# A Winograd convolution whose first unit begins with points 0 and infinity, with the third weight loaded behind the rows

## The chip, the cores and the metric

The kernel runs on one core of a Trainium2 chip. The metric is the device time in microseconds of one launch. The kernel before takes 189.95 us (median of three runs, 189.86 to 190.31).

## The reference

A convolution of width 3 over the sequence, with 1024 channels in and out, for two sequences of 2048 positions, then batch normalization and SiLU. Everything is bf16 in memory.

```python
B, S, C, K = 2, 2048, 1024, 3
xp = jnp.pad(x, ((0, 0), (1, 1), (0, 0)))
y = sum(jnp.einsum('bsc,cd->bsd', xp[:, k:k + S, :], w[k]) for k in range(K))
inv_std = 1.0 / jnp.sqrt(var + 1e-5)
y = (y - mean) * (g * inv_std) + b
return jax.nn.silu(y)
```

## The kernel before

The kernel computes the convolution by a Winograd scheme: six outputs (R) at a time from eight transformed inputs (NJ), one for each of the points 0, 1, -1, 2, -2, 1/2, -1/2 and infinity. A sequence has 342 blocks of six positions (NB). Channels stand in 8 tiles of 128 on either side (CT in, DC out).

**Loading.** SP loads the rows of x in 17 windows of up to 128 rows for each sequence (L486 to L489 and L505), 256 KB each but for the short one that comes first, into 12 buffers. The three weights of output tile 0 (256 KB each: the tap planes 0, 2 and 1 in this order) stand in SP's queue behind windows number 5, 8 and 11 (W0_AT). Eight semaphores serve all loads in turn, and a load waits for the one eight places before it.

**Transform of x.** `t_jobs` makes 25 jobs for a sequence. A job (`t_job`, L270) is a group of matmuls of the rows with the matrix `rm` (L278), which put the eight transformed inputs of some blocks into PSUM, and one cast into `T_sb` in SBUF by ScalarE (L289) or VectorE (L291). Which of the two does it is planned at build time: `clock` and `cost` keep an estimate of when each engine is free, and the job goes to the one that would end first. `ahead` (L491) does all jobs of sequence 0 before the first product; those of sequence 1 are strewn among the products of unit 0 by `Between` (L510), 23 of them after so many products as match their share of columns, and the last two by `rest`.

**Transform of the weights.** For an output tile GpSimd makes three pairs `u`: u0 = e0 ± w1, with e0 = w0 + w2, for the points ±1; u1 = e1 ± 2 w1, with e1 = w0 + 4 w2, for ±2; and u2 = e2 ± 2 w1, with e2 = 4 w0 + w2, for ±1/2. Points 0 and infinity take the raw planes w0 and w2. In tile 0 (`prepare_first`, L208) GpSimd does all sums, and ScalarE scales by 4 and 2; it is called behind job 16 of sequence 0. For the other tiles (`prepare_w`, L192) GpSimd makes e0 and the pairs (L169, L190), ScalarE doubles w1 (L157), and VectorE makes e1 and e2 (L171), handed out by `idle` at set places of a unit.

**Units.** A unit (L300) is one output tile and one sequence; there are 16, in the order (tile 0, sequence 0), (tile 0, sequence 1), (tile 1, sequence 0) and so on, and they use PSUM banks 0 to 3 and 4 to 7 by turns. A unit makes eight products, each of 8 matmuls of 128x342 (`product`, L316, its matmuls at L324). `run` (L380) has the order of the first six: points 1, 2, -1, -2, then 1/2 and -1/2. Behind them ScalarE copies some banks to SBUF (L335, L337), and VectorE combines them (L342): `sd`, then a combine into bank 1, then t0, t1 and t2, and, after the last two products, the combines that leave the six outputs in PSUM and in t1. The products of infinity (`last`) and of point 0 (`first`) are added into banks 3 and 0 at the very end of a unit, in the course of the next unit (`rest`), in which ScalarE also does the SiLU of the unit before. The first unit gets `between.rest` instead. `prepare_w` for the next tile is called within `run`, behind the t combines; the first unit prepares tile 1, which unit 2 is the first to use.

The order on each engine is the order in which the program issues the instructions: each engine works through its own queue, with semaphores between them. Ahead of everything six matmuls on zeros (L74) keep TensorE busy until x arrives.

Of the kernel before, what the change touches and what calls it, by code (L numbers as in the profile page):

```python
# [9 lines left out]
ALU = mybir.AluOpType  # L10
FP32 = mybir.dt.float32
BF16 = mybir.dt.bfloat16
# [3 lines left out]
P = 128  # L16
R = 6
NJ = 8
W0_AT = (5, 8, 11)
W0_USE = 16  # L20
EARLY = 23
XBUFS = 12
WARM = 6
WT = 21

@with_exitstack
def kernel(
# [10 lines left out]
    nc = tc.nc  # L38
    B, S, C = x.shape
    D = w.shape[2]  # L40
    CT, DC = C // P, D // P
    NB = -(-S // R)
# [4 lines left out]
    consts = ctx.enter_context(tc.tile_pool(name="consts", bufs=1))  # L47
# [17 lines left out]
    ps = pspool.tile([P, 8, 512], FP32, name="ps")  # L65
# [2 lines left out]
    rows = consts.tile([4 * DC, P], BF16, name="rows")  # L68
    for q, ap in enumerate((var, g, mean, b)):
        nc.scalar.dma_start(out=rows[q * DC:(q + 1) * DC, :], in_=ap.rearrange("(dc p) -> dc p", p=P))  # L70
    zeros = consts.tile([P, 512], BF16, name="zeros")
    nc.vector.memset(zeros, 0.0)
    for _ in range(WARM):
        nc.tensor.matmul(ps[:, 7], lhsT=zeros[:, 0:P], rhs=zeros, start=True, stop=True)  # L74
# [30 lines left out]

    rm = transform_matrix()

    clock = {"pe": 3500.0, "act": 0.0, "dve": 0.0, "dma": 2600.0}
    cost = {"act": (0.833, 250.0), "dve": (1.042, 215.0)}
    bank_free = {}  # L110

# [3 lines left out]
    def busy(e, size):  # L115
        clock[e] = ends(e, size)
# [4 lines left out]
    def load_x(bi, wi):  # L121
        xw = xpool.tile([P, C], BF16, name="xw")
        lo = max(R * WT * wi - 1, 0)
        hi = min(lo + P, S)
        nc.sync.dma_start(out=xw[0:hi - lo, :], in_=x[bi, lo:hi, :])  # L125
        clock["dma"] += 5.7 * (hi - lo)
        xwin[bi, wi] = xw, clock["dma"]

    w_all = w.rearrange("k (ct p) d -> p k ct d", p=P)
    raw, wts = {}, {}  # L130
# [3 lines left out]
    def load_w(pair, k, half=None):  # L134

        if (pair, "tile") not in raw:
            raw[pair, "tile"] = wpools[pair % 2].tile([P, 3, CT, 2, P], BF16, name=f"wch{pair % 2}")
        wch = raw[pair, "tile"]
        h0, h1 = (0, 2) if half is None else (half, half + 1)
        cols = slice((2 * pair + h0) * P, (2 * pair + h1) * P)  # L140
        nc.sync.dma_start(  # L141
            out=wch[:, k, :, h0:h1].rearrange("p c h d -> p c (h d)"), in_=w_all[:, k, :, cols]
        )
        clock["dma"] += 1200.0 * (h1 - h0)
        for h in range(2):
            raw[2 * pair + h] = wch[:, :, :, h]

    double, sums, act_work, dve_work = {}, {}, [], []

    def idle(work):  # L150
        if work:
            work.pop(0)()

    def double_w(dc, eng):
        t = spool.tile([P, CT, P], BF16, name="w1x2")
        if eng is nc.scalar:
            nc.scalar.mul(t, raw[dc][:, 1], 2.0)  # L157
            busy("act", CT * P)
        else:
            eng.tensor_scalar(t, raw[dc][:, 1], 2.0, 0.0, op0=ALU.mult, op1=ALU.add)  # L160
        double[dc] = t

    def even_part(dc, q, eng, by=None):

        w0, w2 = raw[dc][:, 0], raw[dc][:, 2]
        e = epool.tile([P, CT, P], FP32, name=f"e{q}")
        f, h = (w2, w0) if q == 1 else (w0, w2)
        if q == 0:
            eng.tensor_tensor(e, w0, w2, op=ALU.add)  # L169
        elif eng is nc.vector:  # L170
            eng.scalar_tensor_tensor(out=e, in0=f, scalar=4.0, in1=h, op0=ALU.mult, op1=ALU.add)  # L171
        else:
            t = spool.tile([P, CT, P], BF16, name="w1x2")
            if by is nc.scalar:
                by.mul(t, f, 4.0)
                busy("act", CT * P)
            else:
                by.tensor_scalar(t, f, 4.0, 0.0, op0=ALU.mult, op1=ALU.add)
            eng.tensor_tensor(e, t, h, op=ALU.add)
        if eng is nc.vector:  # L180
            busy("dve", CT * P)
        sums[dc, q] = e

    def transform_w(dc, q, signs=(0, 1)):

        o = double[dc] if q else raw[dc][:, 1]
        if (dc, q) not in wts:
            wts[dc, q] = upool.tile([P, 2, CT, P], BF16, name=f"u{q}")
        for i in signs:
            nc.gpsimd.tensor_tensor(wts[dc, q][:, i], sums[dc, q], o, op=(ALU.add, ALU.subtract)[i])  # L190

    def prepare_w(dc):  # L192

        even_part(dc, 0, nc.gpsimd)
        transform_w(dc, 0)

        def second():
            even_part(dc, 1, nc.vector)
            transform_w(dc, 1)

        def third():
            even_part(dc, 2, nc.vector)
            transform_w(dc, 2)

        act_work.append(lambda: double_w(dc, nc.scalar))
        dve_work.extend((second, third))

    def prepare_first(dc):  # L208

        even_part(dc, 0, nc.gpsimd)  # L210
        transform_w(dc, 0, (0,))
        even_part(dc, 1, nc.gpsimd, nc.scalar)
        double_w(dc, nc.scalar)
        transform_w(dc, 1, (0,))
        transform_w(dc, 0, (1,))
        transform_w(dc, 1, (1,))
        even_part(dc, 2, nc.gpsimd, nc.gpsimd)
        transform_w(dc, 2)

    prm = consts.tile([P, 4, DC], BF16, name="prm")  # L220
    scale = consts.tile([P, DC], FP32, name="scale")
# [78 lines left out]
    class Unit:  # L300
# [64 lines left out]
        def both(self, between, then):  # L365
# [3 lines left out]
            self.product(3, NJ - 1, True, between)  # L369
            self.silu(slice(0, R, R - 1), ps[:, self.b0:self.b0 + 4:3, self.lo:self.hi])  # L370

        def rest(self, between, last=5, first=6):
# [113 lines left out]
    for i, wi in enumerate(order):  # L486
        load_x(0, wi)
        if i in W0_AT:
            load_w(0, (0, 2, 1)[W0_AT.index(i)], 0)  # L489

    def ahead(jobs, job_n):  # L491
        for job in jobs:
            t_job(job, job_n % 4 * 2)
            if job_n == 0:
                first_matrix()
            if job_n == 2:
                params()
            if job_n == 5:
                scales()
            if job_n == W0_USE:  # L500
                prepare_first(0)
            job_n += 1

    ahead(t_jobs(0), 0)
    for wi in order:  # L505
        load_x(1, wi)
    for k in (0, 2, 1):
        load_w(0, k, 1)

    class Between:  # L510


        n = done = cols = 0
        jobs = list(t_jobs(1))
        size = [len(wins) * nct * n for wins, _, n, _, nct in jobs]

        def do(self):
            t_job(self.jobs[self.done], (4, 6, 1)[self.done % 3] if self.done < EARLY else (6, 4)[(self.done - EARLY) % 2])
            self.cols += self.size[self.done]
            self.done += 1  # L520

        def __call__(self):
            self.n += 1
            while self.done < EARLY and self.cols * 4 * CT < min(self.n, 4 * CT) * sum(self.size[:EARLY]):
                self.do()

        def rest(self):
# [3 lines left out]
    between = Between()  # L531
    seq = [(dc, bi) for dc in range(DC) for bi in range(B)]
    late = [nc.sync] * (S // R // P + 1) + [nc.gpsimd]
    before = prev = None
    for i, (dc, bi) in enumerate(seq[:-1]):
        unit = Unit(dc, bi, i % 2 * 4)
        unit.run(
            between, prev.rest(between, *((4, 5) if i >= len(seq) - 3 else (5, 6))) if prev else [(5, between.rest)],
            1 if i == 0 else 2 if i == 2 else dc + 2 if bi == 1 and 0 < dc < DC - 2 else None,
        )  # L540
        if i == 0:
            xwin_scope.close()
# [12 lines left out]
    before.store(late)  # L555
    dc, bi = seq[-1]
# [45 lines left out]
```

## Time and profile before

| | |
|---|---|
| median of 3 runs | 189.95 us |
| the profiled execution | 190.66 us, its span 188.9 us |
| TensorE busy (matmuls) | 177.3 us, 94% of the span |
| VectorE | 155.4 us, 82% |
| GpSimd | 139.7 us, 74% |
| ScalarE | 111.1 us, 59% |
| DMA | 31.72 MB, 168 GB/s on average |
| matmuls of the products, L324 | 816 with u and 272 with the raw planes, 120.9 and 42.5 us busy |

The page gives busy time by engine and by group of instructions (engine, line, operation, tiles), the median time of one, and what ended the idle time before it. PE is TensorE, PEld its weight loads, DVE is VectorE, ACT is ScalarE, POOL is GpSimd, and SPq is the queue of SP. A line of a timeline has the start in us, the length in us, the engine, the line of the code, the operation, its tiles as out<-in with sizes, the count of like instructions that it merges, and, in brackets, how long the engine was idle before it and for whom. A line of the chain of waits has the start, the length and the work or wait. A matmul's row is longer than the spacing of matmuls, since they overlap.

### The profile page before, as it was taken

The page shows a single profiled execution, that of the slowest core. Times are in us where ns is not written, and L with a number is a line of the kernel's source. Part 1 is how long each engine was busy: PE and PEld are TensorE (multiplying, and loading weights), DVE is VectorE, ACT ScalarE, POOL GpSimd, SP SyncE. Part 2 cuts the span into 40 slices and gives each one's busy share as a digit, 9 for nine tenths or more (in the row PEclk, how much of TensorE's full clock was granted, in tenths as well). Part 3 has the DMA queues.
Part 4 walks back from the last instruction along what each step waited for, and adds up shares of the span by engine and source line. Part 5 has one row for each costly group of instructions (what it writes and reads, how often), then busy time and mean ns, then how long its engine had stood idle before and what let it go on. Part 6 is the DMA issues. An engine that isn't in the chain of part 4 may idle for free.

```text
span 188.9 us, 3725 instructions
## 1 busy us (share of the span) xinstructions
PE 177.3 (94%) x1404; PEld 125.2 (66%) x1404; DVE 155.4 (82%) x214; ACT 111.1 (59%) x180; POOL 139.7 (74%) x83
## 2 busy tenths in 40 slices
PE   7767799999999999999999999999999999999981
PEld 3646588776666666666666666666666666669880
DVE  5545978789988899998799989888979997669781
ACT  3777887974547474546545654656455546363790
POOL 3536999984798879999999999889999773020122
PEclk9999999999999999999999999999999999999998
DMA  5999999247053939399669584996595768876935
GB/s 164 295 327 353 371 348 243 45 141 199 17 108 29 182 66 201 111 253 205 114 131 185 113 173 139 225 209 127 116 208 110 155 56 183 154 142 131 202 73 111
DMA packets 86958, 31.72 MB, mean 168 GB/s; under 512 B 73542, under 2 KB 82778, under 8 KB 86940
## 3 DMA queue, kind: packets, MB, share of 16 engines
q1 hardware_dynamic: 85820, 31.24, 74.0%
q10 hardware_dynamic: 864, 0.21, 0.5%
q8 instruction: 11, 0.18, 0.4%
q0 software_dynamic: 256, 0.03, 0.2%
q14 instruction: 7, 0.06, 0.1%
HBM read 14.82 MB, written 8.39 MB: 123 GB/s over the span
## 4 chain that ended last, share of the span: by engine, by line
PE 84%; DMA 9%; DVE 1%; SPq 1%; ACT 1%; issue 1%; ACTq 0%; DVEq 0%
PE ps L324 78%; DMA xw<-in_x_dram 7%; PE ps L278 5%; DMA rows<-in_g_dram 1%; DVE T_sb L291 1%; PE ps L436 1%; SPq L125 1%; ACT T_sb L289 1%; SPq L141 0%; ACTq L70 0%; ACT yT L347 0%; DVEq L597 0%; DVE o L437 0%; DVEq L291 0%
## 5 line engine op out<-in xcount | busy, mean ns | idle before, releaser
L324 PE MATMUL ps<-T_sb,u 128*128 128x342 bf16 (+2 forms) x816 | 120.9, 299 | 0.4 <-ACT T_sb L289 0.4
L324 PEld LDWEIGHTS <-u 128*128 128x128 bf16 x816 | 76.7, 97 | 33.5 <-issue 0.2
L190 POOL TENSOR_TENSOR u<-e,w1x 128x1024 bf16<-128x1024 f32 x32 | 70.3, 2220 | 9.5 <-DVE e L171 9.3
L324 PE MATMUL ps<-T_sb,wch 128*128 128x342 bf16 (+2 forms) x272 | 42.5, 300 | 0.0
L347 ACT ACTIVATE yT<-ps,beta,scale 128x342 bf16<-128x342 f32 (+4 forms) x50 | 33.9, 710 | 11.9 <-PE ps L324 11.8
L342 DVE SCALAR_TENSOR_TENSOR t<-ps,sd 128x684 f32<-128x684 f32 (+2 forms) x51 | 39.1, 821 | 0.6
L190 POOL TENSOR_TENSOR u<-e,wch 128x1024 bf16<-128x1024 f32 x16 | 36.7, 2312 | 1.7 <-DMA wch<-in_w_dram 1.1
L324 PEld LDWEIGHTS <-wch 128*128 128x128 bf16 x272 | 25.7, 97 | 11.5
L335 ACT COPY pc<-ps 128x342 f32<-128x342 f32 (+2 forms) x34 | 14.5, 425 | 31.7 <-PE ps L324 30.9
L291 DVE CAST T_sb<-ps 128x1008 bf16<-128x1008 f32 (+2 forms) x20 | 21.7, 1103 | 11.6 <-PE ps L278 11.2
L278 PE MATMUL ps<-rm,xw 128*128 128x168 bf16 (+2 forms) x272 | 25.9, 239 | 5.3 <-DMA xw<-in_x_dram 4.7
L289 ACT CAST T_sb<-ps 128x1008 bf16<-128x1008 f32 (+2 forms) x30 | 25.2, 873 | 7.3 <-PE ps L278 6.6
L342 DVE SCALAR_TENSOR_TENSOR ps<-ps,t 128x684 f32<-128x684 f32 (+2 forms) x34 | 28.3, 831 | 0.6
L171 DVE SCALAR_TENSOR_TENSOR e<-wch 128x1024 f32<-128x1024 bf16 x14 | 28.7, 2048 | 0.0
L278 PEld LDWEIGHTS <-xw 128*128 128x128 bf16 (+2 forms) x272 | 21.0, 100 | 11.1 <-DMA xw<-in_x_dram 6.5
L342 DVE SCALAR_TENSOR_TENSOR ps<-ps,pc 128x342 f32<-128x342 f32 (+2 forms) x34 | 16.9, 497 | 8.7 <-PE ps L324 5.7
L169 POOL TENSOR_TENSOR e<-wch 128x1024 f32<-128x1024 bf16 x8 | 19.0, 2371 | 4.6 <-DMA wch<-in_w_dram 3.1
L347 ACT ACTIVATE yT<-t,beta,scale 128x684 bf16<-128x684 f32 (+2 forms) x17 | 15.7, 925 | 0.0
L342 DVE SCALAR_TENSOR_TENSOR t<-ps,t 128x684 f32<-128x684 f32 (+2 forms) x17 | 13.9, 818 | 0.0
L335 ACT COPY sd<-ps 128x342 f32<-128x342 f32 (+2 forms) x17 | 7.3, 428 | 10.1 <-PE ps L324 9.7
L337 ACT ACTIVATE pc<-ps 128x342 f32<-128x342 f32 (+2 forms) x17 | 7.5, 440 | 9.8 <-PE ps L324 6.0
L478 POOL DMA_DIRECT2D out_dram<-o x2 | 1.4, 710 | 15.4 <-DMA o<-yT 15.4
(46 smaller groups left out, 49.1 us busy)
## 6 DMA issues: line engine op xcount, KB each, us to landing
xw<-in_x_dram SPq DMA_DIRECT2D x32, 256.0 KB
out_dram<-o SPq DMA_DIRECT2D x28, 192.0 KB
wch<-in_w_dram SPq DMA_DIRECT2D x9, 512.0 KB
out_dram<-o SPq DMA_DIRECT2D x14, 120.0 KB
wch<-in_w_dram SPq DMA_DIRECT2D x6, 256.0 KB
out_dram<-o SPq DMA_DIRECT2D x3, 128.0 KB
o<-yT SPq DMA_TRANSPOSE x15
out_dram<-o SPq DMA_DIRECT2D x12, 7.5 KB
```

The costliest lines, as they stand in the source:

```text
L125: nc.sync.dma_start(out=xw[0:hi - lo, :], in_=x[bi, lo:hi, :])
L169: eng.tensor_tensor(e, w0, w2, op=ALU.add)
L171: eng.scalar_tensor_tensor(out=e, in0=f, scalar=4.0, in1=h, op0=ALU.mult, op1=ALU.add)
L190: nc.gpsimd.tensor_tensor(wts[dc, q][:, i], sums[dc, q], o, op=(ALU.add, ALU.subtract)[i])
L278: nc.tensor.matmul(v[:, q, c], lhsT=xw[0:rows, (c0 + c) * P:(c0 + c + 1) * P], rhs=mat[0:rows, :, 0:n], start=True, stop=True,)
L289: nc.scalar.copy(dst, src)
L291: nc.vector.tensor_copy(dst, src)
L324: nc.tensor.matmul(self.bank[q], lhsT=lhsT, rhs=T_sb[self.bi][:, ct, j, nsl], start=not add and ct == 0, stop=ct == CT - 1, skip_group_che ...
L335: nc.scalar.copy(dst, self.bank[q])
L337: nc.scalar.mul(dst, self.bank[q], by)
L342: nc.vector.scalar_tensor_tensor(out=out, in0=in0, scalar=scalar, in1=in1, op0=ALU.mult, op1=op1)
L347: nc.scalar.activation(self.yT[:, rows, self.lo:self.hi], src, ACT.Silu, bias=beta[:, dc:dc + 1], scale=scale[:, dc:dc + 1])
```

## The change

The third weight plane (w1) of output tile 0 stands in SP's queue behind all rows of sequence 0 instead of behind window 11. `prepare_first` is split. Its first half is called behind job 5: GpSimd makes 4 w0, e0, 4 w2 and e1, which need planes 0 and 2 alone. The rest (`left`: the pairs, the doubling of w1 on ScalarE, and e2) is issued at the start of unit 0.

Unit 0 has an order of its own, `run_first`: its first two products are points 0 and infinity, with raw planes, each copied by ScalarE to an SBUF tile `ends`; then the six others as in `run`. GpSimd adds the two copies onto one half of t0 and of t2, behind VectorE's combines that make these and ahead of `prepare_w` for tile 1. VectorE makes t2 ahead of t1. In unit 1 nothing of unit 0 is left but SiLU work (`rest_first`).

The jobs of sequence 1 follow a table (`at`): the first behind 8 matmuls, then at 12, 14, 16, 18, 20, 22, and the others evenly up to 48. Some figures of the planner differ (3600, 5.4, 1400, T_FIRST). The zeros are fp32, and two matmuls on them take the place of six in bf16.

```diff
-W0_AT = (5, 8, 11)
-W0_USE = 16
+W0_AT = (5, 8, 16)
-WARM = 6
+T_FIRST = 21500.0
+WARM = 2
-    zeros = consts.tile([P, 512], BF16, name="zeros")
+    zeros = consts.tile([P, 512], FP32, name="zeros")
-    clock = {"pe": 3500.0, "act": 0.0, "dve": 0.0, "dma": 2600.0}
+    clock = {"pe": 3500.0, "act": 0.0, "dve": 0.0, "dma": 3600.0}
-        clock["dma"] += 5.7 * (hi - lo)
+        clock["dma"] += 5.4 * (hi - lo)
-        clock["dma"] += 1200.0 * (h1 - h0)
+        clock["dma"] += 1400.0 * (h1 - h0)
     def prepare_first(dc):
-        even_part(dc, 0, nc.gpsimd)
-        transform_w(dc, 0, (0,))
-        even_part(dc, 1, nc.gpsimd, nc.scalar)
-        double_w(dc, nc.scalar)
-        transform_w(dc, 1, (0,))
-        transform_w(dc, 0, (1,))
-        transform_w(dc, 1, (1,))
-        even_part(dc, 2, nc.gpsimd, nc.gpsimd)
-        transform_w(dc, 2)
+        w0, w2 = raw[dc][:, 0], raw[dc][:, 2]
+        g, f = (spool.tile([P, CT, P], BF16, name="w1x2") for _ in range(2))
+        nc.gpsimd.tensor_scalar(f, w0, 4.0, 0.0, op0=ALU.mult, op1=ALU.add)
+        for q, t, h in ((0, w0, w2), (1, g, w0)):
+            if q:
+                nc.gpsimd.tensor_scalar(g, w2, 4.0, 0.0, op0=ALU.mult, op1=ALU.add)
+            sums[dc, q] = epool.tile([P, CT, P], FP32, name=f"e{q}")
+            nc.gpsimd.tensor_tensor(sums[dc, q], t, h, op=ALU.add)
+        def left():
+            transform_w(dc, 0, (0,))
+            double_w(dc, nc.scalar)
+            transform_w(dc, 1, (0,))
+            transform_w(dc, 0, (1,))
+            transform_w(dc, 1, (1,))
+            sums[dc, 2] = epool.tile([P, CT, P], FP32, name="e2")
+            nc.gpsimd.tensor_tensor(sums[dc, 2], f, w2, op=ALU.add)
+            transform_w(dc, 2)
+        return left
+        def run_first(self, between, left, prepare):
...
+            left()
+            self.product(3, 0, False, between)
+            self.copy(3, dst=ends[:, 0])
+            self.product(0, NJ - 1, False, between)
+            self.copy(0, dst=ends[:, 1])
+            clock["pe"] = max(clock["pe"], T_FIRST)
+            self.product(3, 1, False, between)
+            pa = self.copy(3)
+            self.product(0, 3, False, between)
+            pb = self.copy(0, by=4.0)
+            self.product(3, 2, True, between)
+            self.copy(3, dst=sd[:, 0])
+            self.combine(sd[:, 1], pa, 2.0, b3, ALU.subtract)
+            self.product(0, 4, True, between)
+            self.combine(b1, b0, -2.0, pb)
+            for t, a in ((t0, -0.0125), (t2, -0.2), (t1, -0.05)):
+                self.combine(t, self.low, a, sd)
+            nc.gpsimd.tensor_tensor(t0[:, 0], t0[:, 0], ends[:, 0], op=ALU.add)
+            nc.gpsimd.tensor_tensor(t2[:, 1], t2[:, 1], ends[:, 1], op=ALU.add)
+            prepare_w(prepare)
+            self.product(2, 5, False, between)
+            pc = self.copy(2)
+            between.rest()
+            self.product(2, 6, True, between)
+            self.combine(b3, b2, -0.5, pc)
...
+        def rest_first(self):
+            return [
+                (4, self.silu_inner),
+                (5, lambda: self.silu(slice(0, R, R - 1), ps[:, self.b0:self.b0 + 4:3, self.lo:self.hi])),
+            ]
     def ahead(jobs, job_n):
...
             if job_n == 5:
                 scales()
-            if job_n == W0_USE:
-                prepare_first(0)
+                left.append(prepare_first(0))
     class Between:
-        size = [len(wins) * nct * n for wins, _, n, _, nct in jobs]
+        at = [8, 12, 14, 16, 18, 20, 22] + [22 + (6 * CT - 22) * (q + 1) // (EARLY - 7) for q in range(EARLY - 7)]
         def __call__(self):
             self.n += 1
-            while self.done < EARLY and self.cols * 4 * CT < min(self.n, 4 * CT) * sum(self.size[:EARLY]):
+            while self.done < EARLY and self.at[self.done] <= self.n:
                 self.do()
...
-        unit.run(
-            between, prev.rest(between, *((4, 5) if i >= len(seq) - 3 else (5, 6))) if prev else [(5, between.rest)],
-            1 if i == 0 else 2 if i == 2 else dc + 2 if bi == 1 and 0 < dc < DC - 2 else None,
-        )
+        if i == 0:
+            unit.run_first(between, left[0], 1)
+        else:
+            unit.run(
+                between,
+                prev.rest_first() if i == 1 else prev.rest(between, *((4, 5) if i >= len(seq) - 3 else (5, 6))),
+                2 if i == 2 else dc + 2 if bi == 1 and 0 < dc < DC - 2 else None,
+            )
```

More of the change, by code (lines that the diff above doesn't have):

```diff
@@ L370, in both @@
             self.silu(slice(0, R, R - 1), ps[:, self.b0:self.b0 + 4:3, self.lo:self.hi])
+        def run_first(self, between, left, prepare):
+            b0, b1, b2, b3 = self.bank
+            sd = dpool.tile([P, 2, NB], FP32, name="sd")
+            t0 = dpool.tile([P, 2, NB], FP32, name="t0")
+            t2 = dpool.tile([P, 2, NB], FP32, name="t2")
+            ends = dpool.tile([P, 2, NB], FP32, name="ends")
+            self.y23 = t1 = ypool2.tile([P, 2, NB], FP32, name="t1")
+            left()
[23 more added lines that the diff above has]
+            self.combine(b3, b2, -0.5, pc)
+            self.combine(self.low, self.high, -1.6, t0)
+            self.combine(t1, self.high, -0.4, t1)
+            self.combine(self.high, self.high, -0.1, t2)
+            idle(act_work)
+            idle(dve_work)
+        def rest_first(self):
[3 more added lines that the diff above has]
+            ]
         def rest(self, between, last=5, first=6):
@@ L489 @@
             load_w(0, (0, 2, 1)[W0_AT.index(i)], 0)
+    left = []
     def ahead(jobs, job_n):
@@ L510 @@
     class Between:
-        n = done = cols = 0
+        n = done = 0
         jobs = list(t_jobs(1))
-        size = [len(wins) * nct * n for wins, _, n, _, nct in jobs]
+        at = [8, 12, 14, 16, 18, 20, 22] + [22 + (6 * CT - 22) * (q + 1) // (EARLY - 7) for q in range(EARLY - 7)]
         def do(self):
             t_job(self.jobs[self.done], (4, 6, 1)[self.done % 3] if self.done < EARLY else (6, 4)[(self.done - EARLY) % 2])
-            self.cols += self.size[self.done]
             self.done += 1
```

## The prediction

> **What bounds the kernel now.** I read four views in this order: the chain of waits, then the timelines of SP, GpSimd and VectorE over the first 75 us, then TensorE's timeline around units 1 and 2. From the chain of waits:
>
> ```profile
> 13.56 7.16 DMA xw<-in_x_dram
> ...
> 20.76 0.40 PE ps L278 x3
> 21.19 1.01 ACT T_sb L289
> 22.24 0.30 PE ps L324
> ...
> 39.05 137.19 PE ps L324 x960
> ```
>
> Up to 20.72 us the chain is the loading of x; behind that it is TensorE, and from 39.05 us on it is matmuls of L324 with nothing between them. So whatever moves the start of unit 2 moves the end by as much, if no weight comes late. Weights come from GpSimd, whose timeline from 35 to 57 us shows the set for output tile 1:
>
> ```profile
> 35.35 2.14 POOL L169 TENSOR_TENSOR e<-wch 128x1024 f32<-128x1024 bf16 x1
> 37.57 4.23 POOL L190 TENSOR_TENSOR u<-e,wch 128x1024 bf16<-128x1024 f32 x2
> 44.97 4.23 POOL L190 TENSOR_TENSOR u<-e,w1x 128x1024 bf16<-128x1024 f32 x2 [3.17 <-DVE e L171]
> 50.36 4.22 POOL L190 TENSOR_TENSOR u<-e,w1x 128x1024 bf16<-128x1024 f32 x2 [1.16 <-DVE e L171]
> ```
>
> One sum (e, 128x1024) costs 2.1 us and one u half 2.1 us; the set is complete at 54.6. Who needs it, from TensorE's timeline:
>
> ```profile
> 48.17 1.32 PE L324 MATMUL ps<-T_sb,wch 128*128 128x342 bf16 x8
> 49.33 5.97 PE L324 MATMUL ps<-T_sb,u 128*128 128x342 bf16 x40
> ...
> 56.30 1.32 PE L324 MATMUL ps<-T_sb,u 128*128 128x342 bf16 x8
> ```
>
> 49.33 is the start of unit 2, the first user of tile 1; a product of 8 matmuls takes 1.16 us (48.17 to 49.33), so it needs u1+ at 50.5 and its second u2 half at 56.30, 1.7 us after GpSimd has it. That slack is small, and it is where I expect the change to be decided.
>
> **Part 1, the third weight behind the rows.** SP issues a load when the load eight places earlier has landed (its semaphore waits), so SP's rows date landings. Issue at 15.03 stands for the window ahead of the third weight, 16.15 for the weight, 16.82, 17.50 and 18.18 for the windows behind it, and 20.78 for the last window:
>
> ```profile
> 15.03 0.33 SPq L125 DMA_DIRECT2D xw<-in_x_dram  x1
> 16.15 0.33 SPq L125 DMA_DIRECT2D xw<-in_x_dram  x1
> 16.82 0.33 SPq L125 DMA_DIRECT2D xw<-in_x_dram  x1
> ```
>
> The weight takes 1.12 us, a window 0.67. Moved behind all rows, it lets the last five windows land 1.12 earlier: the last at 19.6 instead of 20.72. The weight takes that window's slot and lands at about 20.7, with the same bytes ahead of it; SP's later loads keep their places.
>
> **Part 2, points 0 and infinity first.** No matmul is added: 16 of them (2.32 us) move from units 1 and 2 into the front of unit 0, where they need only raw weights. GpSimd has e0 and e1 ready before the third weight lands (1.04 for each scaling by 4, 2.13 for each sum, done by 18.2), so u0+ comes at 20.8 + 2.1 = 22.9, and the other five u halves and e2 every 2.1 us until 35.5. TensorE needs u0+ only behind 16 products and four jobs, at about 25, and u2 at 37.7: covered. The doubling on ScalarE (1.05) stands behind its last cast and ends near 22.8, also covered.
>
> The end of unit 0's first six products (0, infinity, 1, 2, -1, -2): 13 + 118 transform matmuls at 0.073 (9.6), 8 small ones (0.24), 48 products at 0.145 (6.96) make 16.7 us. Before, the same stretch with 32 products has 14.4 us of work in 20.76 to 36.99, so 1.8 us idle. With T work thinner between products I take 1.3 us idle (0 to 1.8 possible): 19.64 + 16.7 + 1.3 = 37.7. So from here to the end of unit 1, if nothing stalls: 1.16 (first u2 product), 0.7 for ten T matmuls and 0.3 wait for their banks, 1.16, then six products of unit 1 (6.95): unit 2 could start at 48.0, a lead of **1.3 us**.
>
> A new wait takes 0.7 of it: in unit 1 nothing stands any more between the product of point 1/2 and the one of -1/2, which adds into the same bank, so TensorE waits for ScalarE's copy of it (0.45 us, plus the 0.2 a result takes to come out of TensorE, and semaphores). Before, the last product of unit 0 (1.16 us) covered this. Unit 2 starts at 48.7, lead 0.6.
>
> **Part 3, the two adds on GpSimd.** They stand ahead of the preparation of tile 1 (e0, both u0) in GpSimd's queue, and they wait for VectorE's t0 and t2. GpSimd has no other work ready ahead of them. Before, t0 was the first of
>
> ```profile
> 37.04 0.52 DVE L342 SCALAR_TENSOR_TENSOR ps<-ps,pc 128x342 f32<-128x342 f32 x1
> 37.59 2.42 DVE L342 SCALAR_TENSOR_TENSOR t<-ps,sd 128x684 f32<-128x684 f32 x3
> 43.61 1.22 DVE L171 SCALAR_TENSOR_TENSOR e<-wch 128x1024 f32<-128x1024 bf16 x1
> ```
>
> done at 38.5, right behind TensorE's 36.99. In the changed order two casts instead of one stand between sd and this combine. With TensorE at 37.7, the second cast runs 37.9 to 39.1, the combine to 39.55, t0 to 40.45, t2 to 41.25. So GpSimd, idle from 35.5, does the adds at 40.5 and 41.3 (no row has a 342-wide add: the 1024-wide one's 2.13 in proportion gives 0.71, the line through that and the 8-wide one's 0.20 gives 0.83, I take 0.75; the rows themselves, 0.20 and 2.13, are the far ends, 1.1 less and 2.8 more for the pair), and starts e0 at **42.1**, where before it started at 35.35. That GpSimd does not go round a waiting instruction is shown before: it idles 1.16 us ahead of 50.36 for a sum of VectorE, though e0 of tile 2, behind it in the queue, has had its planes since 47.5.
>
> Then, every 2.1 us: e0 to 44.2, u0+ to 46.4. Two of VectorE's sums (L171) now fall among busy GpSimd work, and this costs both. From the timelines of VectorE and GpSimd around 70 us:
>
> ```profile
> 70.38 2.63 DVE L171 SCALAR_TENSOR_TENSOR e<-wch 128x1024 f32<-128x1024 bf16 x1
> ```
> ```profile
> 67.72 4.22 POOL L190 TENSOR_TENSOR u<-e,w1x 128x1024 bf16<-128x1024 f32 x2 [1.29 <-DVE e L171]
> 71.90 3.11 POOL L169 TENSOR_TENSOR e<-wch 128x1024 f32<-128x1024 bf16 x1
> ```
>
> The VectorE sum, 1.22 alone, waits for GpSimd's instruction to end (71.94), takes 1.08 more, and GpSimd's next one is 1.0 longer. VectorE asks for e1 at 45.0 (t1 to 42.0, the combine of 0.5, three of 0.8 to 0.87): it runs 46.4 to 47.5; GpSimd: u0- to 49.55, u1+ to **51.7**. VectorE then has sd, combine and three t (to 50.9), and its e2 runs 51.7 to 52.75; GpSimd: u1- to **54.85**, u2+ to **56.95**, u2- to 59.0.
>
> The Trainium skill (GPSIMD Engine Reference, section Key points) says that GpSimd shares its SBUF interfaces with VectorE and that contention comes from VectorE instructions with two SBUF inputs; it gives no price. The row agrees on which (L171 has two, the t combines have one and run beside GpSimd at 0.87) and adds the price; without a price the sum would be that of rival B.
>
> Unit 2 on TensorE: u0+ 48.7 to 49.9; u1+ waits to 51.8, ends 52.95; u0- to 54.1; u1- waits to 55.0, ends 56.1; u2+ waits to 57.05, ends 58.2; infinity of unit 1 to 59.4; u2- at **59.4**, where it is at 56.30 now: **+3.1 us**. Behind it the next set (tile 2) starts 4.5 later on GpSimd than before, while TensorE is 3.1 later; tile 2's halves had 2.6 us of slack (u2+ at 69.85 for a need at about 72.5), so no further loss.
>
> **Part 4, fp32 zeros.** VectorE's zeroing row is 0.27 us for 256 words a row; 512 words make it 0.53, so the matrix rm comes at 3.5 instead of 3.3, ahead of TensorE's use. Two fp32 matmuls stand for six bf16 ones of 0.43: at least 0.86 us, and if each took the whole 2.74 of the six, 5.5, ending at 7.0. TensorE then owes 2.5 us of jobs that it had done by 6.4, and it sits idle from 8.44 to 10.27 for x: 1.8 us of cover, and it is at full speed by then. Nothing either way. The Trainium skill (FP8 and Floating Point Precision, TensorE Precision Notes) gives true fp32 four passes, so eight of 0.43, an estimate of 3.4 us: nothing by that too.
>
> **Sum.** Lead -1.3, new copy wait +0.7, stalls of unit 2 +1.9, +0.9 and +0.95: +3.1 with the rounding. On the profiled execution, 190.66 us (span 188.9), that is 193.8; on the median of the runs, 189.95, it is **193.1 us**.
>
> **Rivals.**
> A, faster: the set for tile 1 is still in time. Then only the lead counts: 189.95 - 0.6 = 189.4, or 188.7 if the copy wait is hidden too. It decides on u2+ by about 53.4, so on GpSimd starting e0 some 3.5 us earlier, at 38.6. For it: GpSimd is free at 35.5 and the weights land by 35.3. Against it: the adds stand ahead, and t2 cannot be there before 40. 0.10.
> B: VectorE's two sums cost GpSimd nothing (2.1 less): 191.0. Against it: the 3.11 row. 0.15.
> C: the last window does not land earlier, because what holds it is not the weight (it landed 1.73 behind the one before it, where others take 0.67). All of the above is then 1.1 later: 194.2. 0.12. If that lag goes as well, all is 1.05 earlier: 192.0.
> Forecast, 193.1 (192.0 to 193.9, by TensorE's idle of 0 to 1.8, the lag of the last window, and adds of 0.4 to 1.1): 0.55. Later still, by adds near 2.13 (195.9) or a stall I don't see: 0.08.
>
> Range 190.9 to 194.8: it leaves out A, the low part of B and the far end, 0.2 together. About 0.3% (0.6 us) is what can be told from no change: faster 0.10, same 0.03, slower 0.87.
>
> **What would show it.** Right: GpSimd idle from about 35.5 to 40.5 with VectorE named, e0 of tile 1 at about 42, 3.1 us rows among the u that follow, TensorE waiting for GpSimd's u in three places between 49 and 58, and the last x window near 19.6. Wrong: TensorE without gaps in unit 2, e0 near 36, or the first transform matmuls late because of the warm-up.

## The result, and the profile after

| | before | after |
|---|---|---|
| median of 6 runs, us | 190.19 (189.86 to 190.58) | 192.67 (191.84 to 193.09) |
| ratio after / before, 95% interval | | 1.0128 [1.0102, 1.0153] |
| profiled execution, us (span) | 190.66 (188.9) | 192.87 (191.0) |

The kernel became 1.9 to 2.9 us slower; 193.1 was forecast.

The chain of waits of after (start, length, what; in the order of time), where the first matmuls of L336 in unit 0 and all of units 1 and 2 are concerned:

```profile
19.88 0.60 PE ps L336 x3
...
36.83 1.21 DVE T_sb L303
38.04 0.44 DVE ps L354
38.51 0.88 DVE t L354
39.53 0.68 POOL t L410
40.40 0.92 POOL t L411
41.32 2.10 POOL e L169
43.48 3.26 POOL u L190 x2
46.75 1.90 issue
48.65 2.13 POOL u L190
50.83 1.35 PE ps L336 x8
...
53.80 2.13 POOL u L190
55.98 122.33 PE ps L336 x856
```

In before this chain was TensorE alone from 39.05 us on. Now it leaves TensorE at 36.83 for VectorE (a cast, a combine and t0), goes through both adds (L410, L411), e0 and the u halves on GpSimd, and comes back to TensorE for good at 55.98. The front itself is earlier: the first product of L336 starts at 19.88 where it started at 22.24, 2.36 us sooner. So a lead is won and then more than lost.

GpSimd's timeline from 32 to 62 us shows the place (start, length, line and operation; in brackets the idle time ahead and who ended it):

```profile
30.08 4.22 POOL L190 TENSOR_TENSOR u<-e,w1x 128x1024 bf16<-128x1024 f32 x2
39.53 0.92 POOL L410 TENSOR_TENSOR t<-t,ends 128x342 f32<-128x342 f32 x1 [5.23 <-DVE t L354]
40.40 0.92 POOL L411 TENSOR_TENSOR t<-t,ends 128x342 f32<-128x342 f32 x1
41.27 2.13 POOL L169 TENSOR_TENSOR e<-wch 128x1024 f32<-128x1024 bf16 x1
43.48 5.20 POOL L190 TENSOR_TENSOR u<-e,wch 128x1024 bf16<-128x1024 f32 x2
48.65 9.38 POOL L190 TENSOR_TENSOR u<-e,w1x 128x1024 bf16<-128x1024 f32 x4
```

GpSimd stands idle for 5.23 us with the planes of tile 1 that e0 needs at hand (the trace has them landed at 33.80), because the first instruction in its queue is an add that waits for VectorE. The set, complete at 54.6 before, is complete at 58.02. Two u in rows of 2.13 would take 4.26 and four 8.52; the rows say 5.20 and 9.38, so each holds one u that is 0.9 to 1.0 longer (3.12 and 3.11 taken singly). VectorE's two sums of this set show why; each stands across the start of one of those longer u (45.57 and 50.73), and they took 2.89 and 1.93 us:

```profile
43.80 2.89 DVE L171 SCALAR_TENSOR_TENSOR e<-wch 128x1024 f32<-128x1024 bf16 x1
...
49.92 1.93 DVE L171 SCALAR_TENSOR_TENSOR e<-wch 128x1024 f32<-128x1024 bf16 x1
```

And TensorE's timeline from 44 to 60 us, with unit 2 from 47.70 on:

```profile
46.54 2.48 PE L336 MATMUL ps<-T_sb,u 128*128 128x342 bf16 x16 [0.59 <-ACT pc L347]
50.83 2.49 PE L336 MATMUL ps<-T_sb,u 128*128 128x342 bf16 x16 [1.80 <-POOL u L190]
53.90 1.33 PE L336 MATMUL ps<-T_sb,u 128*128 128x342 bf16 x8 [0.58 <-ACT sd L347]
55.98 1.34 PE L336 MATMUL ps<-T_sb,u 128*128 128x342 bf16 x8 [0.75 <-POOL u L190]
57.16 1.32 PE L336 MATMUL ps<-T_sb,wch 128*128 128x342 bf16 x8
58.32 1.32 PE L336 MATMUL ps<-T_sb,u 128*128 128x342 bf16 x8
```

Four gaps: one for ScalarE's copy pc ahead of 46.54, and three in unit 2. The one ahead of 53.90 is put down to a copy of ScalarE; u1- ended only at 53.84, and the chain of waits follows GpSimd there. Product starts are 1.16 us apart without a gap, so the three cost 1.97, 0.75 and 0.92. The second u2 half is used at 58.32, before at 56.30: 2.0 later, and the last matmul of the products starts 2.1 later (185.55 for 183.47). Behind unit 2 nothing more is lost.

### The profile page after: what moved, and what is told of

Its sections match the earlier page's. It is cut to its first block, busy times and chain, and to the rows that moved or that the text cites. A ratio compares the mean times of both kernels' runs of the same rounds, so it can differ in the third digit from the quotient of the medians.

```text
span 191.0 us, 3722 instructions
## 1 busy us (share of the span) xinstructions
PE 178.2 (93%) x1402; PEld 125.0 (65%) x1402; DVE 159.5 (84%) x214; ACT 110.2 (58%) x180; POOL 145.3 (76%) x86
## 4 chain that ended last, share of the span: by engine, by line
PE 76%; POOL 6%; DMA 5%; DVE 5%; issue 3%; SPq 2%; ACT 1%; DVEq 0%; POOLq 0%
PE ps L336 71%; DMA xw<-in_x_dram 5%; PE ps L290 5%; POOL u L190 4%; DVE T_sb L303 4%; SPq L125 2%; POOL e L169 1%; ACT T_sb L301 1%; PE ps L495 1%; POOL t L411 0%; DVE t L354 0%; POOL t L410 0%; ACT yT L359 0%; DVEq L660 0%; DVE ps L354 0%
## 5 line engine op out<-in xcount | busy, mean ns | idle before, releaser
L336 PE MATMUL ps<-T_sb,u 128*128 128x342 bf16 (+2 forms) x816 | 120.7, 299 | 3.7 <-POOL u L190 2.5
L336 PEld LDWEIGHTS <-u 128*128 128x128 bf16 x816 | 76.4, 97 | 37.9 <-POOL u L190 4.2
L336 PE MATMUL ps<-T_sb,wch 128*128 128x342 bf16 (+2 forms) x272 | 43.0, 299 | 0.4 <-ACT T_sb L301 0.4
L190 POOL TENSOR_TENSOR u<-e,wch 128x1024 bf16<-128x1024 f32 x16 | 39.6, 2495 | 1.9 <-DMA wch<-in_w_dram 1.3
L336 PEld LDWEIGHTS <-wch 128*128 128x128 bf16 x272 | 25.6, 97 | 11.8 <-issue 0.7
L171 DVE SCALAR_TENSOR_TENSOR e<-wch 128x1024 f32<-128x1024 bf16 x14 | 32.8, 2341 | 0.0
L290 PE MATMUL ps<-rm,xw 128*128 128x168 bf16 (+2 forms) x272 | 25.3, 235 | 2.5 <-DMA xw<-in_x_dram 1.9
L169 POOL TENSOR_TENSOR e<-wch 128x1024 f32<-128x1024 bf16 x7 | 16.9, 2412 | 0.0
## 6 DMA issues: line engine op xcount, KB each, us to landing
out_dram<-o SPq DMA_DIRECT2D x28, 192.0 KB
```

The lines of the kernel that those rows point to most:

```text
L290: nc.tensor.matmul(v[:, q, c], lhsT=xw[0:rows, (c0 + c) * P:(c0 + c + 1) * P], rhs=mat[0:rows, :, 0:n], start=True, stop=True,)
L336: nc.tensor.matmul(self.bank[q], lhsT=lhsT, rhs=T_sb[self.bi][:, ct, j, nsl], start=not add and ct == 0, stop=ct == CT - 1, skip_group_che ...
```

## The experiments

The theory: the lead is real, and the two adds give more than it away, because they wait for VectorE at the head of GpSimd's queue while e0 of tile 1 stands behind them. Its rivals: the loss comes from the shared work of GpSimd and VectorE (the rows longer by 1.0), from the cost of the adds themselves, from the weight's new place, or from the warm-up. Medians are of 4 to 12 runs; where kernels ran on different chips they are compared by their ratios to before.

| kernel | median, us | ratio to before, 95% interval |
|---|---|---|
| after | 192.67 | 1.0128 [1.0102, 1.0153] |
| x1, adds behind the preparation | 189.94 | 0.9983 [0.9959, 1.0007] |
| x2, adds in the gap within it | 189.37 | 0.9947 [0.9931, 0.9962] |
| x5, adds on VectorE | 190.14 | 0.9996 [0.9981, 1.0012] |
| x6, two more adds on GpSimd | 195.35 | 1.0273 [1.0247, 1.0298] |
| x9, sums of one input | 191.29 | 1.0056 [1.0036, 1.0075] |
| x3, weight back in its old place | 194.55 | 1.0223 [1.0203, 1.0244] |
| x8, before, weight moved alone | 193.01 | 1.0155 [1.0117, 1.0192] |
| x4, bf16 warm-up | 192.57 | 1.0120 [1.0101, 1.0139] |
| x7, point 0 alone up front | 188.55 | 0.9917 [0.9894, 0.9940] |

### x1 and x2: the same adds, elsewhere in the queue

x1 calls `prepare_w` for tile 1 ahead of the two adds:

```diff
+            prepare_w(prepare)
             nc.gpsimd.tensor_tensor(t0[:, 0], t0[:, 0], ends[:, 0], op=ALU.add)
             nc.gpsimd.tensor_tensor(t2[:, 1], t2[:, 1], ends[:, 1], op=ALU.add)
-            prepare_w(prepare)
```

> The changed kernel with one thing moved: GpSimd makes e0 and both u0 halves of tile 1 ahead of the two adds instead of behind them. Theory (the adds hold the queue): GpSimd starts e0 at about 34.8 us, when its planes have landed, not at 41.3; the adds run at about 41.2 and 42.1 and make VectorE's combine onto the low banks some 0.7 to 1.5 us late, which costs nothing; the three waits of TensorE in unit 2 (2.0, 0.75 and 0.9 us in the changed kernel) go to 0 to 0.4 in all, and the time falls by 3.2 to 3.6 us, to 189.1 to 189.5 against 190.2 for the kernel before. Rival 1 (what costs is VectorE's e1 and e2 falling among busy GpSimd work): the waits stay at 2 us or more, 191.5. Rival 2 (the new order of products in itself costs the time): no change, 192.7.

x2 puts them between the first and the second half of u0:

```diff
-    def prepare_w(dc):
+    def prepare_w(dc, mid=None):
...
-        transform_w(dc, 0)
+        if mid:
+            transform_w(dc, 0, (0,))
+            mid()
+            transform_w(dc, 0, (1,))
+        else:
+            transform_w(dc, 0)
...
-            nc.gpsimd.tensor_tensor(t0[:, 0], t0[:, 0], ends[:, 0], op=ALU.add)
-            nc.gpsimd.tensor_tensor(t2[:, 1], t2[:, 1], ends[:, 1], op=ALU.add)
-            prepare_w(prepare)
+            def add_ends():
+                nc.gpsimd.tensor_tensor(t0[:, 0], t0[:, 0], ends[:, 0], op=ALU.add)
+                nc.gpsimd.tensor_tensor(t2[:, 1], t2[:, 1], ends[:, 1], op=ALU.add)
+
+            prepare_w(prepare, add_ends)
```

> The changed kernel with e0 and u0+ of tile 1 ahead of the two adds and u0- behind them. GpSimd was idle from 34.3 to 39.5 us there, and e0 and u0+ fill 34.8 to 39.1, so by the theory the adds stay where they were (39.5 to 41.3) and u0- ends at 43.4; VectorE asks for e1 at 43.8 and finds GpSimd idle, so e1 takes 1.2 instead of 2.9 us. TensorE has no wait for a u half in unit 2, or one of under 0.3 us (u2+). Time 188.9 to 189.3, at most 0.3 below the version with the adds last. Rival 1 (VectorE's sums among GpSimd work): 191.5. Rival 2 (the order of products): 192.7.

Both give the loss back: 0.9983 and 0.9947 stand against 1.0128, 2.8 and 3.4 us less (the difference of the ratios times 190.2). Both medians lie a little above what was expected (189.94 for 189.1 to 189.5, 189.37 for 188.9 to 189.3). GpSimd's timeline of x2, to be laid beside that of after:

```profile
34.38 2.12 POOL L169 TENSOR_TENSOR e<-wch 128x1024 f32<-128x1024 bf16 x1
36.58 2.12 POOL L190 TENSOR_TENSOR u<-e,wch 128x1024 bf16<-128x1024 f32 x1
38.97 0.91 POOL L416 TENSOR_TENSOR t<-t,ends 128x342 f32<-128x342 f32 x1 [0.27 <-DVE t L359]
39.83 0.92 POOL L417 TENSOR_TENSOR t<-t,ends 128x342 f32<-128x342 f32 x1
40.70 2.13 POOL L190 TENSOR_TENSOR u<-e,wch 128x1024 bf16<-128x1024 f32 x1
44.61 4.22 POOL L190 TENSOR_TENSOR u<-e,w1x 128x1024 bf16<-128x1024 f32 x2 [1.77 <-DVE e L171]
49.99 4.22 POOL L190 TENSOR_TENSOR u<-e,w1x 128x1024 bf16<-128x1024 f32 x2 [1.16 <-DVE e L171]
```

The adds cost what they cost in after (0.91 and 0.92), and start within 0.6 us of where they started there. But e0 and one u are done before them, in what was idle time: the wait of 5.23 has become 0.27. No row of GpSimd is longer any more either. VectorE's rows of the same two sums show where that went:

```profile
43.25 1.22 DVE L171 SCALAR_TENSOR_TENSOR e<-wch 128x1024 f32<-128x1024 bf16 x1
...
47.70 2.22 DVE L171 SCALAR_TENSOR_TENSOR e<-wch 128x1024 f32<-128x1024 bf16 x1
```

The first falls into GpSimd's own pause and takes 1.22. The second still stands across the end of a u (48.83) and takes 2.22, as in before (2.23); GpSimd's next u needs its result, so there the time shows as an idle time of 1.16 and not as a longer row. The set is complete at 54.2, TensorE starts unit 2 at 47.15 and waits once in it, 0.22 us (x1 once, 0.56).

Not all that these two profiles gain is the edit's: their front is 0.55 us earlier than after's (the seventh product of unit 0 starts at 36.06 and 36.08 for 36.63), as the last window of x landed 0.6 earlier in them, which the edit does not touch. Within unit 2 the comparison is free of that: from the unit's start to its second u2 product it is 10.62 us in after, 7.71 in x1 and 7.36 in x2, so 2.9 and 3.3 less. The price of the adds is thus not the question; what stood behind them was.

### x5: the adds on VectorE

```diff
-            nc.gpsimd.tensor_tensor(t0[:, 0], t0[:, 0], ends[:, 0], op=ALU.add)
-            nc.gpsimd.tensor_tensor(t2[:, 1], t2[:, 1], ends[:, 1], op=ALU.add)
+            nc.vector.tensor_tensor(t0[:, 0], t0[:, 0], ends[:, 0], op=ALU.add)
+            nc.vector.tensor_tensor(t2[:, 1], t2[:, 1], ends[:, 1], op=ALU.add)
```

> The changed kernel with the two adds on VectorE instead of GpSimd, in the same place of the program. Nothing on GpSimd waits for VectorE ahead of tile 1's e0 then, so by the theory most of the 3.3 us that the version with the adds in the middle gained over the changed kernel (189.4 against 192.7) comes back. But an add has two inputs in SBUF, like the sums of L171, which were seen to wait for GpSimd's instruction: the adds come at a time when GpSimd makes u0 and u0-, so each may wait up to 2.1 us, and VectorE's chain to e1 and e2 moves back by 1 to 2 us, of which TensorE sees 0.4 to 1.2 at u2+. Expected 189.8 to 190.6, and GpSimd's u0 rows longer than 2.13. Without that mutual wait: 189.4. If the adds' queue were not the cause: 192.7 or more.

0.9996: the loss goes, no gain comes. VectorE's timeline of x5 shows the adds:

```profile
40.25 1.23 DVE L410 TENSOR_TENSOR t<-t,ends 128x342 f32<-128x342 f32 x1
41.41 0.50 DVE L411 TENSOR_TENSOR t<-t,ends 128x342 f32<-128x342 f32 x1
```

The second one, with GpSimd at rest, takes 0.50 us; the first waited for GpSimd's u0-, which ended at 41.11. GpSimd's u0 rows stayed at 2.1, where longer ones had been expected, so here only VectorE paid. But VectorE makes e1 and e2 of tile 1 as well, and they are later now; in unit 2 TensorE waits for the u2 made from e2:

```profile
53.64 1.34 PE L336 MATMUL ps<-T_sb,u 128*128 128x342 bf16 x8 [1.47 <-POOL u L190]
```

### x6: more work in the same place

Two more adds, whose sum nobody reads, behind the two:

```diff
+            for _ in range(2):
+                nc.gpsimd.tensor_tensor(ends[:, 0], ends[:, 0], ends[:, 1], op=ALU.add)
```

> The changed kernel with two more adds of 342 columns on GpSimd (on ends, which nothing reads any more) between its two and tile 1's e0. By the theory GpSimd's chain from the adds to u2- is what TensorE waits for in unit 2, so their 1.84 us (2 x 0.92, the row of the changed kernel) come out at the end in full: 194.4 to 194.6. If TensorE's waits were set by VectorE (e1, e2) or by the copies, 192.7 to 193.2.

They take 0.79 each, 1.58 in all, and the time rises by 2.8 us against after (1.0273 against 1.0128), where 1.8 had been expected: a longer queue on GpSimd makes the kernel slower, but the size is not clean. The set itself is complete only 1.1 us later than in after (59.16 for 58.02). Something else is added on TensorE. Its row of unit 2:

```profile
52.98 7.66 PE L336 MATMUL ps<-T_sb,u 128*128 128x342 bf16 x32 [3.82 <-POOL u L190]
```

32 matmuls in 7.66 us are 0.24 each, for 0.145 elsewhere. The table by stretches of x6 has the granted clock in its last column but two (stretch, its length, then busy time of PE, PEld, DVE, ACT and POOL, clock, DMA share, GB/s):

```profile
50.00:53.00 3.00, 0.02 (x1) 0.03 (x2) 2.97 (x5) 0.00 (x0) 3.00 (x2) 0.83 0.46 84
53.00:56.00 3.00, 3.00 (x11) 1.61 (x12) 0.84 (x2) 0.46 (x1) 3.00 (x2) 0.50 0.00 0
56.00:58.00 2.00, 2.00 (x9) 1.05 (x7) 0.00 (x0) 0.20 (x1) 2.00 (x2) 0.50 0.00 0
```

During a wait of 3.82 us the clock fell to half, and stayed there for what followed. In after, with gaps of 1.97 at most, the clock is 1.00 from 48 to 60 us, so this has no part in the loss that is to be explained.

### x9: VectorE's sums from one input

Rival B priced the shared work at nothing. x9 makes VectorE's sums of tile 1 from one plane; it leaves out the other, so its outputs of tile 1 lack that part:

```diff
+        elif eng is nc.vector and dc == 1:
+            eng.tensor_scalar(e, f, 4.0, 0.0, op0=ALU.mult, op1=ALU.add)
```

> The changed kernel, with VectorE's e1 and e2 of tile 1 made by an instruction that reads one tensor instead of two: it scales w0 or w2 by 4 and leaves out the addition of the other plane, so the outputs of tile 1 lack that part. This measures what the meeting of VectorE's sums with busy GpSimd work costs. Theory of the prediction: the one-input form does not wait for GpSimd's instruction and does not lengthen the next one, so GpSimd's chain from 41.3 us is 2.0 us shorter (two rows of 3.1 become 2.13), u2- is ready at 56.0 instead of 58.0, and the time falls by 1.9 to 2.1 us, to 190.6 to 190.8. Rival: what matters is not the second input, and the one-input form meets GpSimd in the same way: rows of 3.1 stay, or they get other lengths, and the time is 192.7 within 0.5.

The time falls by 1.4 us (1.0056 against 1.0128), between what the theory (1.9 to 2.1) and the rival (at most 0.5) had said, and not in the way that a rule of two inputs would have it. VectorE's two rows in x9:

```profile
43.51 2.34 DVE L171 TENSOR_SCALAR e<-wch 128x1024 f32<-128x1024 bf16 x1
...
49.09 1.40 DVE L171 TENSOR_SCALAR e<-wch 128x1024 f32<-128x1024 bf16 x1
```

and GpSimd's rows of the same set:

```profile
43.18 4.67 POOL L192 TENSOR_TENSOR u<-e,wch 128x1024 bf16<-128x1024 f32 x2
47.81 8.85 POOL L192 TENSOR_TENSOR u<-e,w1x 128x1024 bf16<-128x1024 f32 x4
```

An instruction with one input stands across the end of GpSimd's as well (the two that it overlaps end at 45.3 and 49.9), and GpSimd's next one is longer as well: 2.58 taken singly, where the two-input form made it 3.11 and nothing 2.13. So the two exclude each other with one input too, for a shorter time. Of the 1.37 us by which u2- is earlier in this profile (56.95 for 58.32), 1.06 are the shorter rows (4.67 and 8.85 for 5.20 and 9.38) and 0.30 an earlier start of u0+ (43.18 for 43.48). The shared work is thus a real term, of which x9 takes about half. But its size is tied to the queue: in x2, without any edit to VectorE, the longer rows are gone and the first sum meets nobody; the second still waits 1.0 us for GpSimd, as in before, and TensorE sees 0.22 of it.

### x3 and x8: the weight's place

```diff
-W0_AT = (5, 8, 16)
+W0_AT = (5, 8, 11)
```

> The changed kernel with the third weight back behind window 11 (W0_AT 5, 8, 11), all else as changed. By the prediction the last window of sequence 0 lands 1.1 us later (19.4 to 20.7 instead of 18.3), everything behind it moves along, and the time is 1.1 us higher, 193.8. Rival: the casts into T_sb end the wait ahead of the first product anyway (the chain of the changed kernel shows them from 14.9 to 19.8 us), and the time is the same, 192.7 within 0.3.

x3 is after with the weight back at its old place: 1.0223 against 1.0128, 1.8 us more, where 1.1 had been expected. The place is thus a gain, and more than the 1.12 us of the weight's own transfer. SP's rows date the landings of the last two windows; after:

```profile
17.45 0.33 SPq L125 DMA_DIRECT2D xw<-in_x_dram  x1
...
18.40 0.55 SPq L125 DMA_DIRECT2D xw<-in_x_dram  x1
```

and x3:

```profile
18.38 0.75 SPq L125 DMA_DIRECT2D xw<-in_x_dram  x1
...
20.47 0.33 SPq L125 DMA_DIRECT2D xw<-in_x_dram  x1
```

The next to last comes 0.93 earlier in after, near the weight's 1.12. The last comes 2.07 earlier, because it follows the one before it by 0.95 instead of 2.09. The whole unit is shifted with it: x3 starts unit 2 at 49.93 for 47.70 and then has the same three waits (1.78, 0.58, 0.75 in its rows). Less its copy wait of 0.76, that start is 0.16 ahead of before's 49.33, and in after 2.4: the lead comes from the weight's place, and hardly from the order of the products; but x8 shows that the place needs the new order.

x8 makes the reverse edit in before, and nothing else:

```diff
-W0_AT = (5, 8, 11)
+W0_AT = (5, 8, 16)
```

> The kernel before with the third weight behind all rows (W0_AT 5, 8, 16) and nothing else: one part of the change alone. The last window lands 1.1 to 2.0 us earlier (near 18.5 to 19.6 against 20.7), but now u0+ stands between the weight (19.5 to 20.7) and the first product: GpSimd needs 2.1 us, and ScalarE's doubling, ahead of casts in its queue, waits for the weight. By the theory the lead is lost and the time is 190.2 to 191.2, not below the kernel before. If the load order alone were worth its 1.1 us: 189.1.

1.0155, slower by 2.9 us, where at most 1.2 us had been expected. The timeline of x8 from 17 us on:

```profile
20.07 1.06 ACT L157 ACTIVATE w1x<-wch 128x1024 bf16<-128x1024 bf16 x1 [3.12 <-DMA wch<-in_w_dram]
20.18 2.12 POOL L190 TENSOR_TENSOR u<-e,wch 128x1024 bf16<-128x1024 f32 x1 [5.37 <-DMA wch<-in_w_dram]
...
21.79 1.73 PE L278 MATMUL ps<-rm,xw 127*128 127x168 bf16 x16 [3.03 <-DMA xw<-in_x_dram]
```

ScalarE, which also casts T, has the doubling ahead of casts in its queue and stands 3.12 us for the weight; TensorE stops for 3.03. Its row names the DMA of a window, but the last one had landed at 18.06 (SP's row of 18.12); what came last is ScalarE's first cast behind the doubling, which ended at 21.74. Behind this stop the granted clock was 0.64 and 0.51 in 22 to 24 and 24 to 26 us, so a part of the 2.9 us is the clock's; the parts were not measured singly. The wait is the same mistake as that of the adds, on another engine, and the new order of unit 0 is what avoids it: in after the doubling stands behind the last cast of sequence 0, and both late weight and early rows are to be had together.

### x4: the warm-up

```diff
-WARM = 2
+WARM = 6
...
-    zeros = consts.tile([P, 512], FP32, name="zeros")
+    zeros = consts.tile([P, 512], BF16, name="zeros")
```

> The changed kernel with the zeros in bf16 again and six matmuls on them. The first x matmul is back at about 3.9 us from 5.2, the zeroing at 0.27 from 0.5 us. By the prediction this is covered by the idle time of TensorE between 8.4 and 10.1 us: 192.7 within 0.3. Rival: the early matmuls run at a higher clock after the fp32 work (12 of them in 1.33 us instead of 1.85), and bf16 costs 0.5 us: 193.2.

1.0120 [1.0101, 1.0139]: no difference from after's 1.0128 that can be told, and all product starts of units 0 to 2 are within 0.1 us of after's. TensorE's first rows of after:

```profile
1.45 3.78 PE L74 MATMUL ps<-zeros 128*128 128x512 f32 x4 [1.45 <-DVE dummy L76]
5.16 0.50 PE L290 MATMUL ps<-rm,xw 33*128 33x48 bf16 x8
```

The two fp32 matmuls (four rows) took 3.78 us, between the 0.86 and 5.5 that the prediction allowed and 0.4 above its estimate of 3.4. Behind them the first x matmul comes at 5.16, in before at 3.86. The idle time ahead of later windows takes up the 1.3 us, as the prediction had it.

### x7: point 0 alone up front

x2, with the product of infinity and its add back behind unit 0's other products, where it covers the copy of pc, and with the jobs of sequence 1 at even steps among the first 40 matmuls:

```diff
-            self.product(0, NJ - 1, False, between)
-            self.copy(0, dst=ends[:, 1])
...
+            def add_ends():
+                nc.gpsimd.tensor_tensor(t0[:, 0], t0[:, 0], ends[:, 0], op=ALU.add)
+
+            prepare_w(prepare, add_ends)
...
-        def rest_first(self):
+        def rest_first(self, between):
             return [
                 (4, self.silu_inner),
-                (5, lambda: self.silu(slice(0, R, R - 1), ps[:, self.b0:self.b0 + 4:3, self.lo:self.hi])),
+                (5, lambda: self.silu(0, self.bank[0])),
+                (5, lambda: self.last(between)),
             ]
...
-        at = [8, 12, 14, 16, 18, 20, 22] + [22 + (6 * CT - 22) * (q + 1) // (EARLY - 7) for q in range(EARLY - 7)]
+        at = [8] + [8 + (5 * CT - 8) * (q + 1) // (EARLY - 1) for q in range(EARLY - 1)]
...
```

> The version with the adds in the middle, but only point 0 goes to the front of unit 0; infinity stays at the end and runs in unit 1 between the products of 1/2 and -1/2, as in the kernel before, so that there is one add and TensorE has 1.16 us of work while ScalarE copies the bank. The jobs of sequence 1 go at even steps among the first 40 matmuls. By the prediction the copy wait (0.59 us idle in the trace of that version, 0.75 by the spacing of products) goes and one add less (0.92) takes away the 0.2 to 0.4 wait for u2+: 188.4 to 188.8 against its 189.4. Rival: with 8 products fewer in front the casts of sequence 1 are denser and TensorE waits for them, so that it stays at 189.4 or goes above.

0.9917 [0.9894, 0.9940], better than both kernels (188.55 us, where 188.4 to 188.8 was expected). TensorE's timeline of x7 from unit 1's end on has no gap:

```profile
45.55 1.32 PE L341 MATMUL ps<-T_sb,wch 128*128 128x342 bf16 x8
46.71 7.14 PE L341 MATMUL ps<-T_sb,u 128*128 128x342 bf16 x48
53.69 1.32 PE L341 MATMUL ps<-T_sb,wch 128*128 128x342 bf16 x8
```

The raw product at 45.55 (tile wch) stands where after waited for pc; behind it the last u product of unit 1 and the first five of unit 2 run in one piece of 48 matmuls. Whether x7 is better than x2 the runs do not settle: the intervals overlap, the chips differ, and the two profiled spans are 187.5 and 187.3. x7 has no copy wait, but starts unit 2 at 47.87, 0.7 later; in its profile the last window landed 1.2 us later than in x2's (SP's rows 18.98 and 17.78), which the edit does not explain.

## Why the prediction was right

The terms of its sum, against the profile of after:

| step | predicted | measured |
|---|---|---|
| last window of sequence 0 lands | 19.6 | 18.34 |
| from there to unit 0's seventh product | 18.1 | 18.3 (36.63) |
| lead at unit 2, without the copy wait | 1.3 | 2.4 (49.33 less 47.70, and 0.75) |
| copy wait in unit 1 | 0.7 | 0.75 (a row of 0.59) |
| GpSimd idle, then each add | from 35.5 to 40.5; 0.75 | to 39.53, 5.23 long; 0.92 |
| e0 of tile 1 starts | 42.1 | 41.27 |
| e0 to the end of the set | 16.9 | 16.75 |
| stalls of unit 2 | 1.9, 0.9, 0.95 | 1.97, 0.75, 0.92 |
| u2-, against before | +3.1 | +2.0 |

**The stalls and their cause** hold, in size, place and order, and x1 and x2 show the cause and do not only argue it: with the adds moved within one queue, and nothing else changed, 2.9 and 3.3 us of waits in unit 2 go, where the whole loss is 2.5 on the medians. The 1.0 us for each of VectorE's sums was in the rows again (3.12 and 3.11 for 2.13).

**The weight's place** is the term that was mis-sized. I took 1.12 us, the weight's transfer, and let the last window keep its lag of 1.73 behind the one before it. The lag fell to 0.95, and the window landed at 18.34 (SP's row follows the landing by 0.06), 1.26 earlier than forecast. TensorE, VectorE and the adds follow this landing: the seventh product of unit 0 starts 18.3 to 18.5 us behind it in the profiles of after, x1 to x6 and x9, for landings from 17.65 to 20.40. So e0 was 0.8 earlier and the loss 1.1 smaller. The second half of rival C names this case (192.0 for "that lag goes as well"): on the profiled execution 193.8 less 1.05 is 192.75, and 192.87 was measured; on the medians 190.19 and 2.05 are 192.2, and 192.67 was measured.

How near the number came is partly luck: among the nine profiles with the weight behind the rows the landing lies between 17.65 and 18.92, in each of them earlier than the 19.6 of the forecast, and unit 0 moves with it.

The runs put the lag on the last place in this series of loads, not on the window. With the weight behind the rows, the last window follows the one before it by 0.75 to 1.42 in all nine profiles, and in some the weight, now in that place, comes late (1.86 to 2.62 us behind the window in x2, x5, x8 and x9; 1.12 in after). In x3 the window has that place again, and lags by 2.09. The change thus gave the place to a load that is not needed at once: the first product with u starts at 23.98. What makes the lag is open.

**The adds** were priced too low, 0.75 for 0.92 us. Even the line through the two rows, 0.83, was under it; on the way from the first add to e0 this is 0.14 us (1.74 for 1.6, or 41.27 less 39.53 for 42.1 less 40.5).

**Rival A** (the set in time) fell, for the reason given against it; x1 and x2 are what it describes, at 0.4 and 1.0 us below before in the medians (x1's interval holds 1), where it said 0.6. It gave GpSimd 38.6 as the latest start of e0; x1 and x2 start it at 33.91 and 34.38. **Rival B** (no price for VectorE's sums) fell by the rows of after; with about half of that price x9 is 1.4 us faster. The sentence of the Trainium skill that the prediction draws on there (GPSIMD Engine Reference, Key points) names a second case beside two inputs, a 2-port mode of VectorE; whether x9's sums ran in it no run here shows. **Rival C's** first half (no earlier landing) fell by x3. **The warm-up** was worth nothing, by x4.

## What to carry to other kernels

On an engine that works its queue in order, a small instruction that waits holds all that stands behind it: before adding one, look at what is next in that queue and who waits for that, and put the small one behind as much independent work as fits into its wait (x2: the same two adds, 3.4 us). A product that only fills time between another and the one that adds into the same bank is doing a job; if it moves, a copy comes to light (0.75 us, gone again in x7). A load moved back is a gain only if what consumes it moves back in every queue too (x3 against x8).

## What the runs showed of the hardware

- **The granted clock after an idle TensorE.** It was 0.50 from 51.98 to 58.81 us in x6, where TensorE stood idle from 49.16 to 52.98, and from 22.56 to 25.97 in x8, where it was idle from 18.76 to 21.79. So it fell within the first idle time, 2.8 us into it, and 0.8 us behind the end of the second. It stayed at 1.00 through idle times of up to 1.87 us (1.80 in after, 1.87 in before). The Trainium skill (TensorE: Matmul & The Clock Gate, Part 1) puts the limit at an idle window of about 3.4 us that does not start with the gap; here the 3.4 us ahead of either fall were not idle throughout, and 2.8 and 2.65 us of idle time in them were enough.
- **VectorE and GpSimd.** A 128x1024 instruction on VectorE waited for the end of GpSimd's running one also with a single input (x9), and a 128x342 add with two inputs waited as well (1.23 us for 0.50, x5). What VectorE's instruction still took behind that end is, less 0.1, what GpSimd's next row grew by: 1.08 and 0.98 us in after, 0.54 and 0.45 in x9. Where GpSimd's next instruction needed the result, no row grew (x2).
- **A DMA's lag.** The last of a row of equal windows landed 0.95 us behind the one before it in after, 1.73 in before and 2.09 in x3; in the latter two it is the last load of the series. A 16 KB packet of an instruction queue, 1.1 to 1.3 us long, starts between 16.9 and 19.0 us in all eleven profiles, those with the lag and those without, so by itself it does not explain it. The cause is open.
